# A decay table read backwards in place of its copy, other PSUM banks for the first two attention tiles, and a new order of loads and moves

## The chip, the cores and the metric

The kernel runs on one core of one Trainium2 chip. The metric is the device time of one execution in microseconds (us). The core has five instruction queues: PE (matmul), DVE (vector), ACT (scalar), POOL (GpSimd) and SP, which here issues every DMA. Each queue is worked off in order; an instruction waits for the data and the buffers that it needs.

## The reference

Three layers, one behind the other, in float32: an attention with decay, a layer with a gate, and a mixture of experts with soft routing.

```python
# attention: q, k, v are (2, 8, 768, 64), lam is (8,), worked off in blocks
for b in range(nb):
    intra = np.einsum('bhic,bhjc->bhij', qb, kb) * Dmask[None]   # lam ** (i - j) below the diagonal
    intra = np.einsum('bhij,bhjd->bhid', intra, vb)
    inter = np.einsum('bhid,bhde->bhie', qb * lam_pow[None], kv_state)
    out[:, :, sl] = intra + inter
    kv_state = lam_block[None, :, None, None] * kv_state + np.einsum('bhsd,bhse->bhde', kb * rev_pow[None], vb)
# gate: x (1536, 512), w_in (512, 2048), w_out (2048, 512)
h = x @ w_in
g = h * np.clip(h + 3.0, 0.0, 6.0) / 6.0
x = g @ w_out
# soft mixture: phi (512, 32), w1 (8, 512, 1024), w2 (8, 1024, 512); 4 slots an expert
logits = x @ phi
d = softmax of logits over the 1536 tokens;  slot_input = d.T @ x
slot_out[e] = np.maximum(slot_input[e] @ w1[e], 0.0) @ w2[e]
c = softmax of logits over the 32 slots;  out = c @ slot_out
```

## The kernel before

The 1536 tokens are twelve tiles t of 128 (six per batch); two neighbours make a pair tp. The 2048 columns of w_in are four parts n of 512.

*Attention* of a tile: pt are the transposed q and k, which ACT copies to tr; ps are the scores (two banks); DVE multiplies them with the decay table `dec` into pm; px is the output, from pm and v and, but for the first tile of a batch, from trd (q times powers of lam) and the state; pv is the state's increment, from v and from kd, k times the table's last column, which POOL makes. x is px in two parts for exact products.

*The decay table* holds, for each of 128 rows and 8 heads, 128 powers. DVE computes the powers (pw), copies them reversed into rp, SP stores rp to DRAM (pw_d) and reads it back with an offset of one element a row: dec_r (512 KB). ACT then copies dec_r, reversed, to dec.

*The gate*: w_in and w_out come as raw integer pairs (wraw, wo_raw). Two operations on ACT and two on DVE make floats of a block of 128 x 512 (tmp_i, tmp_o; "shift" is the last of them on DVE); for w_in ACT and POOL split them into whi and wlo. h of (t, n) is an h unit: two halves of six matmuls each, the first of which needs the first two k-blocks of part n. ACT and DVE make g of it. w_out times phi becomes w2s: transposes pwo, products w2p, for each n.

*The logits* of a pair and part n are lg, from w2s and from g with its tokens in the other layout. For pairs 0 to 4 the layout is changed by a move: DVE transposes blocks (gb), SP writes them to DRAM (gd, four transfers) and reads them back (gq). For pair 5 PE and ACT do it (pg, gt). All of them wait for every w2s. softmax (lr, dn, pd) collects the token sums as pairs come in; after the last pair psi gives the slots' input, and the experts run: p1 with w1, po with w2, whose weights (e, 64 transfers of 512 KB) SP loads into slots that come free.

*Memory*: 49 slots of 4 KB a partition in SBUF (the ring) hold nearly everything; the eight banks of PSUM are tagged h (2), s (2), x, g, l and d (one each). pt, ps and pv all take s; pwo and pg take g, lg takes l, w2p, pd and psi take d.

*The order* is fixed before the program is built. Every step is an `op` with an engine, a cost, its needs, a priority and the slots that it takes and frees; `Plan.run` goes through time with those costs and issues, on each engine, the ready step of the least priority (within `stick`, one that suits PE's mode). CFG holds the numbers that steer it: `order` (the sequence of h for pairs of tiles and parts n), `loads` (the first loads on SP, which follow each other strictly: q, k, v of a tile; t all three of them; W four blocks of w_in; o a block of w_out; P the store of the powers, D the table, p phi), `lead`, `wlead`, `wo`, `lg`, `sm` (what is added to a priority), `lres`, `pres`, `ares` (slots held back), `depth` (how many logits of earlier moves a block transposition lets stand open), and `eff` (the share of 360 GB/s at which a transfer is counted). The costs and waits in the plan set the order only; at run time an instruction waits for data and buffers.

Of the kernel before, what the change touches and what calls it, by code (L numbers as in the profile page):

```python
# [22 lines left out]
    bydma=(0, 1, 2, 3, 4),  # L23
    mv=-1034.0,
    mres=1,
    depth=6,
    warm=(1, 6, 5),
    order='00 01 10 11 02 03 12 13 20 22 21 23 30 31 32 33 40 41 42 51 43 50 52 53',
    stick=2.75,
    loads='q0 k0 P0 q1 D0 v0 k1 t2 p0 W0 v1 W1 v3 o8 q3 k3 W2 o9 t5 o10 o4 o6 o7 o5 k4 q4 v4 W3 o3 o0 o13 o1 o11 t6 t11 o12 o2 t9 t8 t7 o14 o15 t10',  # L30
    lead=5.5,
    wlead=-3.75,
    wo=7.0,
    lg=-9.5,
    sm=-9.25,
# [161 lines left out]
def attn_moe_softmoe_kernel(  # L197
# [23 lines left out]
    C = 128  # L221
# [23 lines left out]
    def rtile(shape, name, dt=F32):  # L245
        return ring.tile(shape, dt, tag=f"R{plan.slots['R'].pop(0)}", name=name)
# [147 lines left out]

    pw_done = op("DVE", 10, lambda: None, prio=-2000)

    def load_dec():
        T["dec_r"] = rtile([128, H, C], "dec_r")
        SP.dma_start(
            out=T["dec_r"],  # L400
            in_=bass.AP(pw_d.tensor, pw_d.offset, [[1, 128], [2 * C, H], [1, C]]),
        )

    rp_buf = Buf("R", 1, (1,))
    for item in CFG["loads"].split():
        i = int(item[1:])
        if item[0] in "qkv":
            load_qkv(item[0], i)
        elif item[0] == "t":
            for x in "qkv":  # L410
                load_qkv(x, i)
        elif item[0] == "w":
            load_w_in(i // 4, i % 4)
        elif item[0] == "W":
            for kt in range(KT):
                load_w_in(i, kt)
        elif item[0] == "p":
            ops["phi"] = load(load_phi, 65536, eff=0.4)
        elif item[0] == "P":
            ops["pw_d"] = load(store_pw, 8192, deps=[pw_done], rel=[rp_buf])  # L420
        elif item[0] == "D":
            ops["dec_r"] = load(
                load_dec, KB512, deps=[ops["pw_d"]], take=[ring_buf("dec_r")], eff=0.65
            )
        elif item[0] == "o":
            load_wo_raw(i)
        else:
            for kk in range(4 * i, 4 * i + 4):
                load_wo_raw(kk)

    def make_dec():
        T["dec"] = rtile([128, H, C], "dec")
        r = T.pop("dec_r")
        ACT.copy(
            T["dec"], bass.AP(r.tensor, r.offset + C - 1, [list(r.ap[0]), [C, H], [-1, C]])
        )

    def lamq_products():
        T["lamq_p"] = ptile("x", [128, NPAIR, C], "lamq_p")
# [6 lines left out]
    def make_lamq():  # L449
# [179 lines left out]
    def attention(t, prio):  # L632
# [214 lines left out]
    def logits(tp, n, prio):  # L847
# [61 lines left out]
        if tp in BY_DMA:  # L909
# [570 lines left out]
```

## Time and profile before

| | |
|---|---|
| runs | 321.19, 323.36 and 326.72 us, median 323.36 |
| the profiled execution | 323.14 us, span in the profile 321.0 us |
| busy in the span | PE 288.5 us, DVE 180.5, ACT 131.6, POOL 48.9 |
| moved by DMA | 93.30 MB |
| chain of waits, by engine | PE 57%, DMA 23%, DVE 9% |

The span is what the profile covers. A busy PE is one with a matmul in flight; since matmuls are pipelined, the share says where PE stood still and not how fast it was. The chain of waits is followed back from the last instruction, at each step to what released it.

### The profile page before, as it was taken

The page shows a single profiled execution, that of the slowest core. Times are in us where ns is not written, and L with a number is a line of the kernel's source. Part 1 is how long each engine was busy: PE and PEld are TensorE (multiplying, and loading weights), DVE is VectorE, ACT ScalarE, POOL GpSimd, SP SyncE. Part 2 cuts the span into 40 slices and gives each one's busy share as a digit, 9 for nine tenths or more (in the row PEclk, how much of TensorE's full clock was granted, in tenths as well). Part 3 has the DMA queues.
Part 4 walks back from the last instruction along what each step waited for, and adds up shares of the span by engine and source line. Part 5 has one row for each costly group of instructions (what it writes and reads, how often), then busy time and mean ns, then how long its engine had stood idle before and what let it go on. Part 6 is the DMA issues. An engine that isn't in the chain of part 4 may idle for free.

```text
span 321.0 us, 6470 instructions
## 1 busy us (share of the span) xinstructions
PE 288.5 (90%) x2532; PEld 211.7 (66%) x2532; DVE 180.5 (56%) x338; ACT 131.6 (41%) x239; POOL 48.9 (15%) x62
## 2 busy tenths in 40 slices
PE   4667969999999999998899699999999988899782
PEld 3456858888888788886556275776787556566341
DVE  5167899999662264774399636457432516530032
ACT  2258969799555345231223121234233331112032
POOL 5126751352511101200100010000000010000000
PEclk9997999999999999999999899999999999999978
DMA  4999999998859705398889999978989999999977
GB/s 92 234 354 361 327 305 313 387 293 236 221 144 246 205 0 127 77 271 284 273 266 311 302 351 378 372 245 255 317 248 415 418 420 418 418 414 414 383 270 259
DMA packets 76318, 93.30 MB, mean 291 GB/s; under 512 B 41976, under 2 KB 60416, under 8 KB 76288
## 3 DMA queue, kind: packets, MB, share of 16 engines
q1 hardware_dynamic: 76288, 92.89, 86.3%
q8 instruction: 20, 0.33, 0.4%
q14 instruction: 10, 0.08, 0.1%
HBM read 75.04 MB, written 17.83 MB: 289 GB/s over the span
## 4 chain that ended last, share of the span: by engine, by line
PE 57%; DMA 23%; DVE 9%; SPq 4%; issue 3%; ACT 2%; DVEq 0%
PE h L799 31%; DMA e<-in_moe_w_dram 9%; DMA gq<-gd 7%; DMA gd<-gb 5%; PE ps L677 4%; PE px L713 3%; SPq L883 3%; PE lg L903 3%; PE pwo L590 2%; PE px L708 2%; PE pt L646 2%; PE pd L999 2%; DVE gb L874 2%; DMA dec_r<-pw_d 2%; PE pg L856 1%
## 5 line engine op out<-in xcount | busy, mean ns | idle before, releaser
L799 PE MATMUL h<-whi,x 128*128 128x512 f32 x384 | 123.8, 404 | 1.8 <-DVE g L819 1.7
L799 PEld LDWEIGHTS h<-whi,x 128*128 128x128 f32 x384 | 68.4, 188 | 19.7 <-issue 3.6
L799 PE MATMUL h<-wlo,x 128*128 128x512 f32 x192 | 75.3, 392 | 0.0
L813 ACT ACTIVATE g<-h,half_b 128x512 f32<-128x512 f32 x48 | 33.0, 688 | 74.3 <-PE h L799 72.9
L819 DVE SCALAR_TENSOR_TENSOR g<-g,h 128x512 f32<-128x512 f32 x48 | 32.8, 684 | 48.7 <-ACT g L813 47.6
L799 PEld LDWEIGHTS h<-wlo,x 128*128 128x128 f32 x192 | 36.0, 188 | 8.1
L874 DVE STREAM_TRANSPOSE gb<-g 128x1024 f32<-128x1024 f32 x20 | 24.6, 1236 | 6.0 <-PE px L713 3.0
L529 POOL TENSOR_TENSOR wlo<-tmp_i,whi 128x512 fp32r<-128x512 f32 x16 | 21.6, 1360 | 27.4 <-ACT whi L526 27.3
L731 POOL TENSOR_TENSOR state<-state,lamq 64x256 f32<-64x256 f32 x16 | 10.2, 639 | 89.2 <-PE px L708 60.0
L685 DVE TENSOR_TENSOR pm<-ps,dec 128x512 f32<-128x512 f32 x24 | 15.7, 683 | 13.5 <-PE ps L677 7.8
L677 PE MATMUL ps<-tr 64*128 64x128 f32 x192 | 16.7, 323 | 3.9 <-ACT tr L657 3.9
L677 PEld LDWEIGHTS ps<-tr 64*128 64x128 f32 x192 | 14.1, 222 | 8.1 <-ACT tr L657 5.1
L657 ACT COPY tr<-pt 128x512 f32<-128x512 f32 x24 | 13.8, 593 | 13.3 <-PE pt L646 9.1
L502 DVE SCALAR_TENSOR_TENSOR tmp_i<-tmp_i 128x512 int32<-128x512 int32 x16 | 16.9, 1064 | 2.2 <-ACT tmp_i L488 2.1
L903 PE MATMUL lg<-gq,w2s 128*32 128x256 f32 x160 | 13.1, 401 | 4.9 <-DMA gq<-gd 4.8
L1333 PE MATMUL po<-e,ht 128*32 128x256 f32 x256 | 15.9, 397 | 1.3 <-DMA e<-in_moe_w_dram 1.3
L646 PE MATMUL pt<-ident,qk 128*128 128x128 f32 x96 | 15.6, 300 | 1.3 <-DVE pm L685 1.1
L713 PE MATMUL px<-pm,vd 128*64 128x128 f32 x192 | 14.6, 292 | 2.4 <-DVE pm L685 2.4
L666 POOL TENSOR_TENSOR vd<-qk,dec 128x512 f32<-128x512 f32 x10 | 11.8, 1182 | 25.1 <-DMA qk<-in_k_dram 17.5
L1299 PE MATMUL p<-e,sim 128*32 128x256 f32 x256 | 14.2, 380 | 1.3 <-DVE sim L1182 1.3
L646 PEld LDWEIGHTS pt<-ident,qk 128*128 128x128 f32 x96 | 11.9, 153 | 4.8 <-issue 2.1
L713 PEld LDWEIGHTS px<-pm,vd 128*64 128x64 f32 x192 | 11.2, 143 | 4.3 <-DVE pm L685 3.0
(107 smaller groups left out, 349.0 us busy)
## 6 DMA issues: line engine op xcount, KB each, us to landing
e<-in_moe_w_dram SPq DMA_DIRECT2D x64, 512.0 KB, 9.7
gd<-gb SPq DMA_DIRECT2D x80, 128.0 KB, 4.6
gq<-gd SPq DMA_DIRECT2D x20, 512.0 KB, 5.1
wraw<-in_moe_w_in_dram SPq DMA_DIRECT2D x16, 512.0 KB, 5.9
wo_raw<-in_moe_w_out_dram SPq DMA_DIRECT2D x16, 512.0 KB, 7.7
wo_d<-wo_f SPq DMA_DIRECT2D x32, 128.0 KB, 2.4
wo<-wo_d SPq DMA_DIRECT2D x8, 512.0 KB, 7.2
qk<-in_q_dram SPq DMA_DIRECT2D x12, 256.0 KB, 4.4
```

Source lines behind the costliest of these rows:

```text
L502: DVE.scalar_tensor_tensor(out=lw if dst is None else dst(), in0=hp, scalar=3, in1=lw, op0=ALU.logical_shift_left, op1=ALU.bitwise_or,)
L529: POOL.tensor_tensor(out=T["wlo", n, kt // 2][:, kt % 2], in0=T.pop(("tmp", key))[:, 1].bitcast(F32), in1=T["whi", n, kt // 2][:, kt % 2]. ...
L646: PE.transpose(p[:, a], x[:, i, 2 * a : 2 * a + 2].rearrange("p a d -> p (a d)"), ident,)
L677: PE.matmul(ps[g][:, p], lhsT=y[r, 1, p], rhs=y[r, 0, p], start=True, stop=True)
L685: DVE.tensor_tensor(out=T["pm", t].rearrange("p (a g) c -> p g a c", g=2)[:, g], in0=T["ps", t][g], in1=T["dec"].rearrange("p (a g) c -> p ...
L713: PE.matmul(px[64 * h2 : 64 * h2 + 64, p], lhsT=vd[:, 0, h], rhs=P[:, h], start=c == 0, stop=c == 0 or p == NPAIR - 1,)
L799: PE.matmul(ph, lhsT=xt[:, a, kt], rhs=T[w, n, part][:, kt % 2], start=i == 0, stop=i == 3 * KT - 1,)
L813: ACT.activation(T["g", tp, n][:, i], T["h", t, n], AF.Relu, bias=half_b, scale=1.0 / 6.0)
L819: DVE.scalar_tensor_tensor(out=to, in0=to, scalar=1.0, in1=T.pop(("h", t, n)), op0=ALU.min, op1=ALU.mult,)
L874: DVE.transpose(out=x.rearrange("p q c i t -> p i c q t"), in_=T["g", tp, n].rearrange("p i (c q t) -> p i c q t", c=4, q=4),)
L903: PE.matmul(T["l", tp][32 * c4 : 32 * c4 + 32], lhsT=w2s[:, n, c4], rhs=rhs, start=n == 0, stop=n == NF - 1,)
L1333: PE.matmul(T["po", hf][32 * qd : 32 * qd + 32], lhsT=T["ht", e // 4][:, e % 4, b8], rhs=T["e2", e, b8 // 2][:, b8 % 2, lo:hi] if e < WHOL ...
```

## The change

The table is read where it lands: dec_r becomes dec, and `T["dec"]` is an access pattern over it that runs backwards, so that DVE (pm) and POOL (kd) read it with a negative step; ACT's copy and its slot are gone. For tiles 0 and 1 (`early=2`) pt of q, pt of k and pv take the banks g, l and d in place of s. The moves' `eff` become 0.72 and 0.98, `depth` 3, and the numbers in CFG others, among them `order` (n = 3 of tiles 4 and 5 earlier) and `loads`.

```diff
@@ -23,24 +23,25 @@
     bydma=(0, 1, 2, 3, 4),
     mv=-1034.0,
     mres=1,
-    depth=6,
+    depth=3,
     warm=(1, 6, 5),
...
-    loads='q0 k0 P0 q1 D0 v0 k1 t2 p0 W0 v1 W1 v3 o8 q3 k3 W2 o9 t5 o10 o4 o6 o7 o5 k4 q4 v4 W3 o3 o0 o13 o1 o11 t6 t11 o12 o2 t9 t8 t7 o14 o15 t10',
...
+    loads='q0 k0 P0 k1 v0 q1 D0 p0 W0 v1 t2 W1 v3 o8 q3 k3 W2 o9 o10 W3 o4 o6 o7 o5 k4 t5 q4 v4 o3 o0 o13 o1 t6 o12 o2 o11 t9 t7 t8 o14 o15 t10 t11',
...
-    ahead=17,
+    ahead=0,
     whole=6,
     ares=0,
+    early=2,
 )
 
 
@@ -394,12 +395,13 @@
 
     pw_done = op("DVE", 10, lambda: None, prio=-2000)
 
+
     def load_dec():
-        T["dec_r"] = rtile([128, H, C], "dec_r")
+        r = rtile([128, H, C], "dec")
         SP.dma_start(
-            out=T["dec_r"],
-            in_=bass.AP(pw_d.tensor, pw_d.offset, [[1, 128], [2 * C, H], [1, C]]),
-        )
+            out=r, in_=bass.AP(pw_d.tensor, pw_d.offset, [[1, 128], [2 * C, H], [1, C]])
+        )
+        T["dec"] = bass.AP(r.tensor, r.offset + C - 1, [list(r.ap[0]), [C, H], [-1, C]])
 
     rp_buf = Buf("R", 1, (1,))
     for item in CFG["loads"].split():
@@ -419,8 +421,8 @@
         elif item[0] == "P":
             ops["pw_d"] = load(store_pw, 8192, deps=[pw_done], rel=[rp_buf])
         elif item[0] == "D":
-            ops["dec_r"] = load(
-                load_dec, KB512, deps=[ops["pw_d"]], take=[ring_buf("dec_r")], eff=0.65
+            ops["dec"] = load(
+                load_dec, KB512, deps=[ops["pw_d"]], take=[ring_buf("dec")], eff=0.5
             )
         elif item[0] == "o":
             load_wo_raw(i)
@@ -429,14 +431,6 @@
                 load_wo_raw(kk)
 
 
-
-
-    def make_dec():
-        T["dec"] = rtile([128, H, C], "dec")
-        r = T.pop("dec_r")
-        ACT.copy(
-            T["dec"], bass.AP(r.tensor, r.offset + C - 1, [list(r.ap[0]), [C, H], [-1, C]])
-        )
 
     def lamq_products():
         T["lamq_p"] = ptile("x", [128, NPAIR, C], "lamq_p")
@@ -456,11 +450,6 @@
         "DVE", 600, make_lamq, deps=[ops["lamq_p"]], prio=-9, rel=[b_x],
         take=[ring_buf("lamq")],
     )
-    ops["dec"] = op(
-        "ACT", 950, make_dec, deps=[ops["dec_r"]], prio=-10, rel=[bufs["dec_r"]],
-        take=[ring_buf("dec")],
-    )
-
 
 
 
@@ -635,12 +624,15 @@
         prev = ops.get(("state", t - 1)) if c > 0 else None
         old, new = states[c % 2], states[(c + 1) % 2]
         b_tr, b_trd, b_pm = Buf("R"), Buf("R"), Buf("R")
-        b_q, b_k, b_s, b_v, b_x = Buf("s"), Buf("s"), Buf("s", 2), Buf("s"), Buf("x")
+
+        q_tag, k_tag, v_tag = "gld" if t < CFG["early"] else "sss"
+        b_q, b_k, b_v = Buf(q_tag), Buf(k_tag), Buf(v_tag)
+        b_s, b_x = Buf("s", 2), Buf("x")
         b_qk, b_vd = bufs["qk", t], bufs["vd", t]
 
         def f_tr(i):
             def fn():
-                p = T["pt", t, i] = ptile("s", [128, NPAIR, C], f"pt{t}_{i}")
+                p = T["pt", t, i] = ptile((q_tag, k_tag)[i], [128, NPAIR, C], f"pt{t}_{i}")
                 x = T["qk", t]
                 for a in range(NPAIR):
                     PE.transpose(
@@ -692,7 +684,7 @@
 
         def f_pv():
             vd = T["vd", t]
-            pv = T["pv", t] = ptile("s", [128, NPAIR, D], f"pv{t}")
+            pv = T["pv", t] = ptile(v_tag, [128, NPAIR, D], f"pv{t}")
             for h in range(H):
                 p, h2 = divmod(h, 2)
                 PE.matmul(
@@ -915,8 +907,8 @@
                 take=[b_gb], reserve=move_reserve,
             )
             ops["gb"] = o
-            o = load(f_move_out, KB512, [o], rel=[b_gb], n=4, prio=CFG["mv"], eff=0.82)
-            o = load(f_move_in, KB512, [o], take=[b_last], prio=CFG["mv"], eff=1.08)
+            o = load(f_move_out, KB512, [o], rel=[b_gb], n=4, prio=CFG["mv"], eff=0.72)
+            o = load(f_move_in, KB512, [o], take=[b_last], prio=CFG["mv"], eff=0.98)
         else:
             b_last, o = b_gt, None
             for i in range(2):
```

What that does to the order, at the places of which the prediction speaks. The first is the start. In these rows pt1_0 is q of tile 1, the last number in a name is the build's own. On SP, before, from the store of the powers to the first block of w_in:

```order
L393 DMA pw_d_90<-rp_77 8x256
L351 DMA qk1_141<-in_q_dram 128x8x64
L399 DMA dec_r_155<-pw_d_90 128x8x128
L351 DMA vd0_159<-in_v_dram 128x8x64
L351 DMA qk1_141<-in_k_dram 128x8x64
L351 DMA qk2_173<-in_q_dram 128x8x64
L351 DMA qk2_173<-in_k_dram 128x8x64
L351 DMA vd2_176<-in_v_dram 128x8x64
L390 DMA phi_b_127<-in_moe2_phi_dram 128x4x32
L364 DMA wraw0_0_179<-in_moe_w_in_dram 128x1024
```

and now:

```order
L394 DMA pw_d_90<-rp_77 8x256
L352 DMA qk1_141<-in_k_dram 128x8x64
L352 DMA vd0_143<-in_v_dram 128x8x64
L352 DMA qk1_141<-in_q_dram 128x8x64
L401 DMA dec_158<-pw_d_90 128x8x128
L391 DMA phi_b_127<-in_moe2_phi_dram 128x4x32
L365 DMA wraw0_0_164<-in_moe_w_in_dram 128x1024
```

k of tile 1 and v of tile 0 stand ahead of the table, and tile 2 behind w_in. On PE, before, behind the scores of tile 0:

```order
L677 MATMUL ps0_1_164<-tr0_157 128x128
L713 MATMUL px0_203<-pm0_193,vd0_159 64x128 x8
L698 MATMUL pv0_216<-vd0_159 64x64 x8
L646 MATMUL pt1_0_230<-ident_91,qk1_141 128x128 x4
L646 MATMUL pt1_1_246<-ident_91,qk1_141 128x128 x4
L677 MATMUL ps1_0_261<-tr1_239 128x128
```

and now:

```order
L669 MATMUL ps0_1_167<-tr0_160 128x128
L638 MATMUL pt1_0_187<-ident_91,qk1_141 128x128 x4
L638 MATMUL pt1_1_194<-ident_91,qk1_141 128x128 x4
L690 MATMUL pv0_223<-vd0_143 64x64 x8
L705 MATMUL px0_238<-pm0_216,vd0_143 64x128 x8
L669 MATMUL ps1_0_254<-tr1_201 128x128
```

The transposes of tile 1 stand ahead of pv and px of tile 0. The second place is the first moves, right behind the last w2s. On DVE, before (gb0_1 is pair 0, n = 1):

```order
L874 STREAM_TRANSPOSE gb0_0_1469<-g0_0_505 128x2x4x4x32
L744 TENSOR_TENSOR state0_123<-state0_123,pv7_1444 64x4x64 x2
L874 STREAM_TRANSPOSE gb0_1_1485<-g0_1_586 128x2x4x4x32
L724 TENSOR_TENSOR x7_1487<-px7_1456,x7_1487 128x512
L874 STREAM_TRANSPOSE gb0_2_1508<-g0_2_846 128x2x4x4x32
L819 SCALAR_TENSOR_TENSOR g2_3_1506<-g2_3_1506,h4_3_1418 128x512
L874 STREAM_TRANSPOSE gb0_3_1522<-g0_3_1023 128x2x4x4x32
L874 STREAM_TRANSPOSE gb1_0_1532<-g1_0_557 128x2x4x4x32
```

and now:

```order
L866 STREAM_TRANSPOSE gb0_0_1434<-g0_0_445 128x2x4x4x32
L866 STREAM_TRANSPOSE gb0_1_1442<-g0_1_588 128x2x4x4x32
L866 STREAM_TRANSPOSE gb0_2_1457<-g0_2_790 128x2x4x4x32
L811 SCALAR_TENSOR_TENSOR g2_2_1390<-g2_2_1390,h5_2_1423 128x512
L811 SCALAR_TENSOR_TENSOR g2_1_1484<-g2_1_1484,h4_1_1449 128x512
L866 STREAM_TRANSPOSE gb0_3_1492<-g0_3_935 128x2x4x4x32
L736 TENSOR_TENSOR state0_123<-state0_123,pv7_1494 64x4x64 x2
L716 TENSOR_TENSOR x7_1503<-px7_1471,x7_1503 128x512
L811 SCALAR_TENSOR_TENSOR g2_1_1484<-g2_1_1484,h5_1_1507 128x512
L866 STREAM_TRANSPOSE gb1_0_1565<-g1_0_648 128x2x4x4x32
```

Three blocks follow each other; g, the state and x stand between the later ones. On SP, before, from the first move on:

```order
L883 DMA gd0_0_1474<-gb0_0_1469 32x4x256 x4
L351 DMA vd10_1491<-in_v_dram 128x8x64
L883 DMA gd0_1_1501<-gb0_1_1485 32x4x256 x4
L883 DMA gd0_2_1517<-gb0_2_1508 32x4x256 x4
L890 DMA gq0_0_1535<-gd0_0_1474 128x1024
L883 DMA gd0_3_1543<-gb0_3_1522 32x4x256 x4
L890 DMA gq0_1_1570<-gd0_1_1501 128x1024
L883 DMA gd1_0_1575<-gb1_0_1532 32x4x256 x4
L883 DMA gd1_1_1589<-gb1_1_1549 32x4x256 x4
L890 DMA gq0_2_1611<-gd0_2_1517 128x1024
L890 DMA gq0_3_1620<-gd0_3_1543 128x1024
```

and now:

```order
L875 DMA gd0_0_1444<-gb0_0_1434 32x4x256 x4
L875 DMA gd0_1_1465<-gb0_1_1442 32x4x256 x4
L875 DMA gd0_2_1486<-gb0_2_1457 32x4x256 x4
L882 DMA gq0_0_1505<-gd0_0_1444 128x1024
L875 DMA gd0_3_1516<-gb0_3_1492 32x4x256 x4
L882 DMA gq0_1_1530<-gd0_1_1465 128x1024
L882 DMA gq0_2_1532<-gd0_2_1486 128x1024
L882 DMA gq0_3_1563<-gd0_3_1516 128x1024
L875 DMA gd1_0_1574<-gb1_0_1565 32x4x256 x4
L875 DMA gd1_1_1604<-gb1_1_1588 32x4x256 x4
```

The reads of n = 1, 2 and 3 of pair 0 stand in a row, ahead of the blocks of pair 1.

## Rows read from the trace of the kernel before

**Rows 1.** The page's 40 slices of the span, busy tenths of PE and of DMA.
```profile
PE   4667969999999999998899699999999988899782
...
DMA  4999999998859705398889999978989999999977
```

**Rows 2.** Stretches of 10 us: length, busy us (instructions) of PE, PEld, DVE, ACT, POOL; PE clock, DMA, GB/s.
```profile
0.00:10.00 10.00, 4.70 (x22) 4.11 (x24) 4.39 (x13) 2.66 (x4) 4.49 (x19) 1.00 0.49 115
10.00:20.00 10.00, 6.92 (x58) 5.58 (x56) 3.51 (x6) 3.10 (x5) 3.19 (x4) 1.00 1.01 270
20.00:30.00 10.00, 6.44 (x58) 5.43 (x58) 7.16 (x12) 8.45 (x15) 4.84 (x5) 0.83 1.07 395
...
40.00:50.00 10.00, 7.25 (x45) 5.34 (x44) 9.91 (x16) 7.09 (x13) 4.90 (x5) 1.00 1.02 326
...
70.00:80.00 10.00, 10.00 (x79) 8.26 (x77) 9.83 (x18) 10.00 (x19) 1.99 (x3) 1.00 0.86 245
```

**Rows 3.** Waits of PE: for whom, us in total, times, longest.
```profile
PE lg L903 <- DMA gq<-gd: 4.8, 4, 2.8
...
PE h L799 <- DVE g L819: 1.7, 1, 1.7
```

**Rows 4.** Timeline of the start: start us, us, engine, line, operation, [idle before it, releaser].
```profile
4.51 1.15 DVE L278 COPY rp<-pw 8x128 f32<-8x128 f32 x1
4.59 1.00 POOL L310 MEMSET state<- 128x512 f32 x2
...
11.87 1.04 ACT L437 COPY dec<-dec_r 128x1024 f32<-128x1024 f32 x1 [2.68 <-DMA dec_r<-pw_d]
12.95 1.29 DVE L685 TENSOR_TENSOR pm<-ps,dec 128x512 f32<-128x512 f32 x2 [5.55 <-ACT dec L437]
...
15.11 1.99 SPq L364 DMA_DIRECT2D wraw<-in_moe_w_in_dram  x4
...
17.05 2.03 PE L646 MATMUL pt<-ident,qk 128*128 128x128 f32 x8
...
19.60 0.68 ACT L481 ACTIVATE tmp_i<-wraw 128x512 f32<-128x512 f32 x1
...
30.46 0.73 PE L799 MATMUL h<-whi,x 128*128 128x512 f32 x2
```

**Rows 5.** Groups of DVE on the page: line, operation, count | busy us, mean ns.
```profile
L685 DVE TENSOR_TENSOR pm<-ps,dec 128x512 f32<-128x512 f32 x24 | 15.7, 683 | 13.5 <-PE ps L677 7.8
...
L502 DVE SCALAR_TENSOR_TENSOR tmp_i<-tmp_i 128x512 int32<-128x512 int32 x16 | 16.9, 1064 | 2.2 <-ACT tmp_i L488 2.1
```

**Rows 6.** o14 and o15: issue and last shift (timeline), first pwo behind (chain).
```profile
104.55 2.75 SPq L378 DMA_DIRECT2D wo_raw<-in_moe_w_out_dram  x2
...
119.01 0.69 DVE L502 SCALAR_TENSOR_TENSOR wo_f<-tmp_o 128x512 int32<-128x512 int32 x1
...
121.65 0.44 PE pwo L590 x4
```

**Rows 7.** Two moves (timeline), and pieces of PE work (chain of waits).
```profile
131.62 1.20 DVE L874 STREAM_TRANSPOSE gb<-g 128x1024 f32<-128x1024 f32 x1
...
144.78 0.64 PE L903 MATMUL lg<-gq,w2s 128*32 128x256 f32 x8
...
166.69 1.24 DVE L874 STREAM_TRANSPOSE gb<-g 128x1024 f32<-128x1024 f32 x1
...
183.02 1.08 PE L903 MATMUL lg<-gq,w2s 128*32 128x256 f32 x8 [2.80 <-DMA gq<-gd]
...
251.50 1.39 PE h L799 x6
...
253.47 1.72 PE pd L999 x16
```

**Rows 8.** The expert stream: SP's issues (timeline), the last DMA piece of the chain.
```profile
240.15 19.20 SPq L1085 DMA_DIRECT2D e<-in_moe_w_dram  x17
...
295.24 8.65 DMA e<-in_moe_w_dram
```

More of the change, by code (lines that the diff above doesn't have):

```diff
@@ L25 @@
     mres=1,
-    depth=6,
+    depth=3,
     warm=(1, 6, 5),
-    order='00 01 10 11 02 03 12 13 20 22 21 23 30 31 32 33 40 41 42 51 43 50 52 53',
-    stick=2.75,
-    loads='q0 k0 P0 q1 D0 v0 k1 t2 p0 W0 v1 W1 v3 o8 q3 k3 W2 o9 t5 o10 o4 o6 o7 o5 k4 q4 v4 W3 o3 o0 o13 o1 o11 t6 t11 o12 o2 t9 t8 t7 o14 o15 t10',
[L31 to L35, printed above, removed]
+    order='00 01 10 11 02 03 23 12 13 20 22 21 30 31 32 33 40 41 42 51 43 50 52 53',
+    stick=1.75,
+    loads='q0 k0 P0 k1 v0 q1 D0 p0 W0 v1 t2 W1 v3 o8 q3 k3 W2 o9 o10 W3 o4 o6 o7 o5 k4 t5 q4 v4 o3 o0 o13 o1 t6 o12 o2 o11 t9 t7 t8 o14 o15 t10 t11',
+    lead=4.5,
+    wlead=-1.5,
+    wo=8.0,
+    lg=-9.0,
+    sm=-11.25,
     lres=4,
-    pres=4,
+    pres=3,
     sto=-1069.0,
```

## The prediction

> **What bounds the kernel now.** I read the strip of 40 slices first, then the table of 10 us stretches, PE's waits, and the timeline of the places where PE stands still. In the strip [rows 1] PE is at 9 from the seventh slice on with few dips, and the DMA engines are at 9 in the last quarter. So the run has three parts: a start in which PE waits, a long stretch in which it hardly does, and a tail paced by the expert weights. The stretches size the first part: PE is busy 4.70, 6.92 and 6.44 us of the first three times 10 us, so 11.94 us are idle, and 2.75 more from 40 to 50 [rows 2]. Behind that the named waits are small: 4.8 us for moved g tiles in front of logits, and 1.7 us for a bank of h that DVE had not emptied [rows 3]. From 240 us on SP issues the last 49 expert transfers without a pause (17 in the row shown, 24 and 8 behind them), and the DMA part of the chain of waits ends with one that lands at 303.9 [rows 8]. That stream starts behind the move of g of the fifth tile pair, so it moves with PE's progress up to there; its length is bytes over a rate that is flat already. I take it that what PE gains ahead of about 236 us comes off the end, one for one, and that nothing else does.
>
> The run profiled took 323.14 us, its span 321.0: 2.1 us lie around it. The median of the runs is 323.36, so I work on 323.1 without a correction. The runs shown spread over 5.5 us; some 2% (6.5 us) is what a measurement of this kernel can tell from no change.
>
> **The copy of the decay table.** It took ACT 1.04 us, and pm of tile 0 started as it ended, at 12.95 [rows 4]. Alone, its removal is worth up to 1.08 us there (11.87 to 12.95). But the order of the loads takes it back: k1 and v0 now stand ahead of the table on SP, two transfers of 256 KB. The stretch from 10 to 20 us moved 270 GB/s [rows 2], so 0.52 MB are 1.9 us more before it lands. Estimate: pm of tile 0 starts at 12.95 - 1.1 + 1.9, near 13.7. Nobody pays these 0.8 us in full: tile 1's transposes now run on PE in the meantime (below).
>
> What reading backwards costs on DVE no row of a like instruction shows. The nearest for the operation is pm itself, 683 ns for 512 columns [rows 5]; for the direction, on ACT, the copy of the table, 1024 columns in 1.04 us. The only backward read on DVE is the copy into rp: 128 columns in 1.15 us [rows 4], 9 ns a column, which would make 512 columns 4.6 us. POOL's memsets of state run beside it, and it ends at 5.66, just behind their end at 5.59, so I read it as a wait and take 0 for each of the 24 pm; the other end is +3.9 us each.
> The Trainium skill (SBUF — State Buffer, section Who interferes with whom) has a rule that fits: a DVE copy in a two-port mode and a GpSimd instruction hold the shared ports for a whole instruction, and the later one blocks; a DVE instruction with one SBUF input outside those modes does not contend. By that rule the long row is the wait, and pm, with ps in PSUM, stays at 0.68 us; by the bare row the sum would grow by tens of us. The row's end agrees; the page Vector Engine (DVE) Microarchitecture Reference, section 5.1, lists operands with a negative step as not measured.
>
> **The start: banks, and the order of the loads.** Today tile 1's transposes follow px and pv of tile 0, since pt, ps and pv share two banks of one kind. They start at 17.05, 4.1 us after pm could begin [rows 4]. With banks g, l and d they stand right behind ps of tile 0, in the hole while the decay table is waited for. Those banks belong to wo's transposes, the logits and w2p, which in PE's order come only after h units of tiles 0 to 3, so I cost that at nothing; were one still in use, PE would wait for one eviction.
>
> The larger part is W0. Its four transfers are issued from 15.11, and ACT starts on the first at 19.60; the first h starts at 30.46 [rows 4], behind POOL's second wlo. Now q2, k2 and v2 stand behind W0: 0.79 MB less ahead of it, at 270 GB/s 2.9 us. So ACT starts near 16.7. From there to the first h it is 10.9 us today, with pt, ps and px of tiles 1 and 2 between; the new order puts ps of tile 2 behind the first two halves of h, and ACT has tile 1's two copies behind it by then. Bounds for this stretch: the 10.9 as it is, or about 8 us, which is eleven ACT operations of some 0.7 us (0.68 the one shown). So the first h stands between 24.7 and 27.6, a gain of 2.9 to 5.8 us.
>
> Whether it stays is up to DVE, busy 9.9 and 9.8 of 10 us in stretches between 40 and 80 [rows 2]. What DVE can win is what it idles between 10 and 30 us, 6.49 + 2.84 = 9.3 us; with pm at 13.7 some 3 us of it pass before it can start, so 6.3 are the upper end. Its shifts take 1064 ns in the mean, where pm with as many columns takes 683 [rows 5]: a share of that is waiting, and it does not go away. I take 4.5 us for the whole start, nearest to the middle of 2.9 and 5.8, with the 1.7 us wait for h inside it. The lower end is 1.5: DVE holds what it has.
>
> **wo, W3 and the order of h.** Counted in h units (12 matmuls, 2.8 us), w2p of n = 3 now comes after 21 and not 22.5 of them, so the logits can start 4.2 us earlier in PE's work. By itself that gains nothing, since units only change places with logits. W3 is loaded ahead of six other loads, at no cost that I see. But o14 and o15 keep their place late on SP, behind the same stores and loads: issued at 104.55, the last converted at 119.70, with pwo of n = 3 at 121.65 [rows 6]. PE would now reach that pwo at 121.65 - 4.2 - 4.5 = 113.0. If the conversion moves with all that stands ahead of it, nothing is late; if it stays, PE waits 6.7 us. The loads ahead are fed by slots that earlier work frees, so I take 0.5.
>
> **The moves of g.** depth and the new rates act on the order alone; at run time only data and buffers are waited for. Blocks of n = 0, 1 and 2 of the first pair now follow each other on DVE and the reads of n = 1, 2 and 3 on SP, where blocks of the next pair stood between. Today the first move takes from 131.62 to 144.78, 13.2 us; a slow one takes from 166.69 to 183.02, 16.3 us, and PE waits 2.80 for it [rows 7]. In the new order the PE work between the logits of one pair and those of the same n of the next, added up from halves of h at 1.39, pd at 1.72 and shorter pieces [rows 7], is 12 us in two places (n = 0 of pairs 0 and 1, n = 3 of 1 and 2), 14 to 17 in six, 20 and more behind. At 13.2 a move plus some 1.5 until DVE comes to it, waits remain at the short gaps, 2 to 3 us each, less where the first has already spread them: some 4, against 4.8 now. I take a gain of 0.5; the bounds are +4.8 (all waits gone) and, at 16.3 + 2 a move in all eight gaps (14.5 in the mean, two rounds of 3.8 us), 7.6 - 4.8 = 2.8 us of loss. `ahead` does nothing, since the reserve that it switches on is of 0 slots.
>
> **Sum.** 323.1 - 4.5 + 0.5 - 0.5 = 318.6 us.
>
> **Rivals.**
> *DVE holds the start back.* For: it is all but full from 40 to 80 with the same work. Against: it idles 9.3 us before. The start gives 1.5 and the moves nothing, 321.6; slow moves on top would give 324.4.
> *The waits for moves go as well.* For: fewer blocks queue on SP ahead of a read. Against: two gaps of only 12 us. 323.1 - 4.5 - 4.8 = 313.8.
> *o15 comes late.* For: its place on SP is unchanged, and PE gets there 8.7 us earlier. Against: its slots come earlier too. At the full price, 323.1 - 4.5 - 0.5 + 6.7 = 324.8, slower than before; it decides from 5 us of wait at that pwo on.
> *Backward reads are slow on DVE.* About 12 of the 24 pm fall where DVE is the bound: 12 x 3.9 = 47 us, 365 and up. For: the row of rp. Against: the memsets beside it, and ACT's row.
>
> **Chances.** Forecast (315.5 to 321) 0.50, DVE holds 0.18, waits go as well 0.19, o15 late 0.10, slow reads 0.03. The range of 311.5 to 324.5 leaves out the slow rivals at their price and the far end of the good one. Faster by over 2% means under 316.9: the third case and a third of the forecast, 0.35; slower by over 2% the last case and what o15 and slow moves could make together, 0.06; the rest 0.59.
>
> **What would show it.** pm of tile 0 near 13.7 at 0.68 us; tile 1's transposes ahead of tile 0's px; ACT's first activation on wraw near 16.7 and the first h between 24.7 and 27.6; PE's idle time of the first 50 us down from 14.7 to about 10; waits for gq near 4 us; no wait at pwo; the pauseless expert stream some 4.5 us earlier at an equal rate. I am wrong if pm is longer, if PE has new waits between 50 and 130 us, or if the end does not follow PE.

## The result, and the profile after

The changed kernel takes 312.85 us in the median of 4 runs (311.09 to 314.37), the kernel before 324.24 beside it (321.19 to 326.72, 4 runs). The ratio is 0.9677 with a 95% interval of 0.9579 to 0.9775: faster, by 10.5 us. The ratio leaves out the run of 326.72 us, a slow one; the medians as they stand differ by 11.4. In a second set of runs (e12 below) the ratio was 0.9627 (0.9583 to 0.9671). The profiled execution took 311.09 us, with a span of 309.3 against 321.0.

The 40 slices of the changed kernel, PE and DMA, to be laid beside [rows 1]:

```profile
PE   4689899999999999998999999999999988899972
DMA  3999999999879761787899999948999999999987
```

From the third slice to the 38th PE is at 8 or 9, where the third and the sixth were at 6, and the dip to 6 at the 23rd slice of [rows 1] is gone. The stretches say the same in numbers (length, busy us of PE, PEld, DVE, ACT, POOL, PE clock, DMA, GB/s), beside [rows 2]; the last line spans the whole stage of the moves:

```profile
0.00:10.00 10.00, 4.70 (x22) 4.10 (x24) 4.39 (x13) 2.66 (x4) 4.48 (x19) 1.00 0.54 123
10.00:20.00 10.00, 8.23 (x71) 7.01 (x68) 4.93 (x9) 5.27 (x9) 2.37 (x3) 1.00 1.04 324
20.00:30.00 10.00, 8.95 (x78) 7.20 (x79) 9.93 (x15) 7.90 (x15) 8.31 (x7) 1.00 0.98 303
30.00:40.00 10.00, 9.12 (x85) 7.20 (x84) 9.57 (x16) 9.70 (x18) 7.79 (x8) 1.00 1.05 361
40.00:50.00 10.00, 9.63 (x68) 7.60 (x67) 8.60 (x17) 9.84 (x18) 3.61 (x5) 1.00 1.02 414
...
130.00:250.00 120.00, 118.73 (x860) 81.79 (x857) 69.11 (x136) 33.62 (x65) 3.71 (x6) 1.00 0.92 322
```

PE's idle time in the first 50 us fell from 14.7 to 9.4 us. From 130 to 250 us it idles 1.3 us and the granted clock is 1.00 throughout. The same stretch of the kernel before:

```profile
130.00:250.00 120.00, 115.09 (x848) 81.04 (x846) 69.55 (x128) 30.29 (x58) 4.77 (x7) 0.99 0.88 296
```

There it was 4.9 us idle, and one ten of these us ran at a mean clock of 0.83, a loss of 1.7 us more.

The start in the timeline of the changed kernel, beside [rows 4]:

```profile
4.51 1.15 DVE L279 COPY rp<-pw 8x128 f32<-8x128 f32 x1
...
11.99 1.94 PE L638 MATMUL pt<-ident,qk 128*128 128x128 f32 x8 [0.67 <-DMA qk<-in_q_dram]
...
14.34 1.28 DVE L677 TENSOR_TENSOR pm<-ps,dec 128x512 f32<-128x512 f32 x2
...
15.40 0.67 ACT L470 ACTIVATE tmp_i<-wraw 128x512 f32<-128x512 f32 x1 [0.84 <-DMA wraw<-in_moe_w_in_dram]
...
24.89 0.71 PE L791 MATMUL h<-whi,x 128*128 128x512 f32 x2
```

Tile 1's transposes stand at 11.99 in place of 17.05 and fill the wait for the table; the first h is 5.6 us earlier. The two groups of [rows 5], from the page of the changed kernel, now with the table read backwards:

```profile
L677 DVE TENSOR_TENSOR pm<-ps,dec 128x512 f32<-128x512 f32 x24 | 15.7, 682 | 6.3 <-PE ps L669 6.0
...
L491 DVE SCALAR_TENSOR_TENSOR tmp_i<-tmp_i 128x512 int32<-128x512 int32 x16 | 15.2, 955 | 0.1
```

PE's waits (for whom, us in total, times, longest), beside [rows 3]:

```profile
PE lg L895 <- DMA gq<-gd: 1.3, 1, 1.3
PE pt L1394 <- DVE r L1377: 1.1, 1, 1.1
PE pv L690 <- POOL vd L658: 1.1, 1, 1.1
```

The waits for moved g went from 4.8 to 1.3 us. No wait of PE for pwo of n = 3 is among them. The moves and what follows, in the timeline, beside [rows 7]:

```profile
121.51 1.08 PE L595 MATMUL w2p<-wo_t,phi_b 128*32 128x128 f32 x32
...
134.99 1.24 DVE L866 STREAM_TRANSPOSE gb<-g 128x1024 f32<-128x1024 f32 x1
...
136.27 0.64 PE L895 MATMUL lg<-gq,w2s 128*32 128x256 f32 x8
...
142.82 0.64 PE L895 MATMUL lg<-gq,w2s 128*32 128x256 f32 x8 [1.27 <-DMA gq<-gd]
...
149.52 0.64 PE L895 MATMUL lg<-gq,w2s 128*32 128x256 f32 x8
...
260.06 3.70 PE L1153 MATMUL psi<-wo,ant 128*32 128x128 f32 x128 [0.18 <-DVE ant L1131]
```

And the expert stream on SP, beside [rows 8]; it starts 9.8 us earlier:

```profile
230.39 19.29 SPq L1077 DMA_DIRECT2D e<-in_moe_w_dram  x17
```

To split the gain I use three landmarks of each timeline: the end of the last w2p (n = 3), where the moves begin; the start of psi, where all logits are done; the end of the span. Because the order sets how many h units stand ahead of that w2p (22.5 before, 21 now), its time is also given for 21 units, at 2.8 us a unit.

| kernel | first h | w2p ends | for 21 units | psi starts | w2p (21) to psi | psi to end |
|---|---|---|---|---|---|---|
| before | 30.46 | 131.31 | 127.1 | 269.73 | 142.6 | 51.3 |
| changed | 24.89 | 122.59 | 122.6 | 260.06 | 137.5 | 49.2 |

So the start gave 4.5 us and the stage of the moves 5.1. The last column differs by 2.0. In this one execution of the kernel before the granted clock was 0.57 in the mean from 305 to 309 us, which is 1.7 us lost; in the 11 runs below in which the column was read it is 49.2 to 50.7, in those with the old order of the moves too. I leave it out, and 9.6 us remain, near the 10.5 of the ratio.

### The profile page after: what moved, and what is told of

The parts are those of the page before. It is cut to its first block, busy times and chain, and to the rows that moved or that the text cites. A ratio compares the mean times of both kernels' runs of the same rounds, so it can differ in the third digit from the quotient of the medians.

```text
span 309.3 us, 6464 instructions
## 1 busy us (share of the span) xinstructions
PE 285.8 (92%) x2532; PEld 212.9 (69%) x2532; DVE 178.7 (58%) x338; ACT 130.9 (42%) x238; POOL 50.8 (16%) x62
## 4 chain that ended last, share of the span: by engine, by line
PE 62%; DMA 12%; SPq 8%; DVE 8%; ACT 4%; issue 3%; POOL 2%; DVEq 0%; ACTq 0%; POOLq 0%
PE h L791 32%; DMA e<-in_moe_w_dram 6%; PE lg L895 4%; PE pd L991 4%; PE ps L669 3%; SPq L352 3%; PE px L705 3%; PE pt L638 3%; DMA gd<-gb 2%; PE px L700 2%; PE pwo L579 2%; SPq L1101 2%; DMA wraw<-in_moe_w_in_dram 2%; PE p L1291 2%; DMA gq<-gd 2%
## 5 line engine op out<-in xcount | busy, mean ns | idle before, releaser
L791 PEld LDWEIGHTS h<-whi,x 128*128 128x128 f32 x384 | 68.4, 188 | 21.5 <-issue 4.0
L518 POOL TENSOR_TENSOR wlo<-tmp_i,whi 128x512 fp32r<-128x512 f32 x16 | 22.7, 1428 | 20.8 <-ACT whi L515 15.9
L649 ACT COPY tr<-pt 128x512 f32<-128x512 f32 x24 | 13.7, 592 | 16.5 <-PE pt L638 14.8
L658 POOL TENSOR_TENSOR vd<-qk,dec 128x512 f32<-128x512 f32 x10 | 12.6, 1259 | 39.0 <-DMA qk<-in_k_dram 12.9
L669 PEld LDWEIGHTS ps<-tr 64*128 64x128 f32 x192 | 13.7, 210 | 4.5 <-issue 2.9
L1325 PE MATMUL po<-e,ht 128*32 128x256 f32 x256 | 14.8, 381 | 0.6 <-DMA e<-in_moe_w_dram 0.6
L491 DVE SCALAR_TENSOR_TENSOR tmp_i<-tmp_i 128x512 int32<-128x512 int32 x16 | 15.2, 955 | 0.1
L638 PEld LDWEIGHTS pt<-ident,qk 128*128 128x128 f32 x96 | 12.1, 154 | 4.5 <-issue 2.5
L491 DVE SCALAR_TENSOR_TENSOR wo_f<-tmp_o 128x512 int32<-128x512 int32 x16 | 11.7, 742 | 4.2 <-ACT tmp_o L477 4.0
L1291 PEld LDWEIGHTS p<-e,sim 128*32 128x32 f32 x256 | 12.0, 110 | 3.1 <-DVE sim L1174 1.6
```

The lines of the kernel that those rows point to most:

```text
L491: DVE.scalar_tensor_tensor(out=lw if dst is None else dst(), in0=hp, scalar=3, in1=lw, op0=ALU.logical_shift_left, op1=ALU.bitwise_or,)
L518: POOL.tensor_tensor(out=T["wlo", n, kt // 2][:, kt % 2], in0=T.pop(("tmp", key))[:, 1].bitcast(F32), in1=T["whi", n, kt // 2][:, kt % 2]. ...
L638: PE.transpose(p[:, a], x[:, i, 2 * a : 2 * a + 2].rearrange("p a d -> p (a d)"), ident,)
L669: PE.matmul(ps[g][:, p], lhsT=y[r, 1, p], rhs=y[r, 0, p], start=True, stop=True)
L791: PE.matmul(ph, lhsT=xt[:, a, kt], rhs=T[w, n, part][:, kt % 2], start=i == 0, stop=i == 3 * KT - 1,)
L1291: PE.matmul(p1[32 * j : 32 * j + 32], lhsT=T["sim"][:, e, b4], rhs=T["e1", e, b4][:, 256 * j : 256 * j + 256], start=b4 == 0, stop=b4 == 3,)
```

## The experiments

The runs e1 to e4, e5 to e8 and e9 to e12 shared a chip each, with runs of the kernel before on it. The table gives medians, the ratio to the kernel before, and the landmarks of the profiled execution (21 h units stand ahead of the last w2p in all but e3 with 21.5, e5 with 20.5 and e9 with 20).

| run | us | ratio, 95% | first h | w2p ends, 21 units | psi | w2p to psi |
|---|---|---|---|---|---|---|
| e1 moves undone | 321.08 | 0.9891 (0.9809 to 0.9973) | 23.94 | 122.6 | 269.81 | 147.3 |
| e2 moves alone | 320.95 | 0.9865 (0.9768 to 0.9962) | | | | |
| e3 banks undone | 318.33 | 0.9807 (0.9727 to 0.9887) | 31.03 | 126.8 | 266.11 | 139.3 |
| e4 loads alone | 324.72 | 1.0007 (0.9969 to 1.0046) | 22.73 | 129.8 | 273.41 | 143.6 |
| e5 banks alone | 325.72 | 1.0061 (1.0025 to 1.0097) | 30.63 | 132.2 | 274.56 | 142.4 |
| e6 rates undone | 317.34 | 0.9777 (0.9704 to 0.9849) | 24.18 | 123.6 | 268.10 | 144.5 |
| e7 depth undone | 311.79 | 0.9625 (0.9568 to 0.9682) | 24.12 | 123.6 | 259.95 | 136.4 |
| e8 loads first | 311.22 | 0.9609 (0.9548 to 0.9670) | 23.01 | 122.7 | 258.95 | 136.3 |
| e9 banks and loads | 319.24 | 0.9835 (0.9782 to 0.9888) | 27.90 | 123.8 | 268.36 | 144.6 |
| e10 copy back | 315.50 | 0.9717 (0.9666 to 0.9768) | 27.96 | 125.2 | 262.36 | 137.2 |
| e11 e8 with depth 6 | 311.24 | 0.9582 (0.9539 to 0.9624) | 23.84 | 123.8 | 260.57 | 136.7 |
| e12 changed, again | 312.55 | 0.9627 (0.9583 to 0.9671) | 24.59 | 123.1 | 260.93 | 137.8 |

One number of the CFG changes the whole plan behind the place where it first matters, so each of these kernels is another order, not the same one with one step taken out; that holds for every difference below. The three sets ran on different chips, so small differences between them are read from the ratios.

My theory after the result was that the gain is two halves: the start, as forecast, and the order of the moves, which I had put at 0.5. The rival was that the waits of the moves went because everything ahead of them had become earlier.

### e1: depth and rates of the moves undone

```diff
-    depth=3,
+    depth=6,
-            o = load(f_move_out, KB512, [o], rel=[b_gb], n=4, prio=CFG["mv"], eff=0.72)
-            o = load(f_move_in, KB512, [o], take=[b_last], prio=CFG["mv"], eff=0.98)
+            o = load(f_move_out, KB512, [o], rel=[b_gb], n=4, prio=CFG["mv"], eff=0.82)
+            o = load(f_move_in, KB512, [o], take=[b_last], prio=CFG["mv"], eff=1.08)
```

> The changed kernel with the old depth and rates of the moves (depth 6, eff 0.82 and 1.08); everything up to the first moves is issued in the changed kernel's order, so the first logits should stand near 136 us as there. Theory (the rates and the depth, by the order of the moves that they give, bring some 5 us of the gain, the start the other 5): 317 to 319 us, with the waits of logits for gq back at 3 to 5 us and stretches of PE at the lower granted clock or idle behind 140 us. Rival (the waits for the moves went because everything ahead of the moves is earlier and stands otherwise, whatever the depth): 312 to 314 us, as the changed kernel.

321.08 us. The start is as in the changed kernel (w2p ends at 122.55), and psi is 9.7 us later. The rival falls: with all else early, the old numbers of the moves give 147.3 us from w2p to psi, more than the kernel before. Its stage of the moves, and two of its stretches:

```profile
130.00:250.00 120.00, 113.07 (x811) 77.91 (x806) 66.95 (x134) 30.20 (x60) 3.70 (x6) 0.99 0.90 314
...
222.00:223.00 1.00, 0.54 (x8) 0.16 (x8) 0.00 (x0) 0.00 (x0) 0.00 (x0) 1.00 0.97 368
...
224.00:226.00 2.00, 2.00 (x10) 1.51 (x8) 1.29 (x2) 0.00 (x0) 0.00 (x0) 0.50 0.67 188
```

PE is idle for 6.9 us. What a wait can do beside its own length is in the timeline of this kernel, at the longest wait for a gq:

```profile
222.46 0.64 PE L895 MATMUL lg<-gq,w2s 128*32 128x256 f32 x8 [2.35 <-DMA gq<-gd]
223.03 1.62 PE L669 MATMUL ps<-tr 64*128 64x128 f32 x16
224.58 1.22 PE L791 MATMUL h<-whi,x 128*128 128x512 f32 x2
...
231.12 0.73 PE L791 MATMUL h<-whi,x 128*128 128x512 f32 x2
```

Two matmuls of h take 1.22 us right behind it and 0.73 later: the granted clock is 0.50, which is 1.2 GHz, from 224 to 226, and the ten us from 220 stand at 0.83 in the mean, 1.7 us lost.

### e2: depth and rates alone

The reverse edit of e1 on the kernel before.

> The kernel before with the new depth and rates of the moves alone (depth 3, eff 0.72 and 0.98), start unchanged: first h near 30.5 us, first logits near 144.8. Theory (the moves' order brings some 5 us by itself): 318 to 320 us, waits for gq 1 to 2 us in all, expert stream issued some 4 to 5 us earlier than 240. Rival (it does nothing without the earlier start and the new order of h): 322 to 325 us, waits for gq near 5.

320.95 us, 0.9865: the numbers of the moves give 4.4 us by the ratio without anything else (1.2 to 7.5 by its interval), near the theory's 5. Of this kernel only the time is used, since its profiled execution, 324.42 us, is the longest of its four.

### e6 and e7: which of the two numbers

e6 is the changed kernel with eff 0.82 and 1.08, e7 with `depth=6`.

> The changed kernel with the old rates of the moves (eff 0.82 and 1.08) and depth 3 kept. If the rates make the order that loses no time to the moves: 318 to 321 us, psi 6 to 9 us behind the changed kernel's 260.1, as in e1. If the depth makes it: 312 to 314, psi near 260 to 261.

> The changed kernel with depth 6 again and the new rates kept. If the depth makes the order that loses no time to the moves: 318 to 321 us, psi 6 to 9 us behind 260.1. If the rates make it: 312 to 314. If each gives a part: both this and e6 between 314 and 318.

e6 takes 317.34 us, e7 311.79. With the new rates, depth is worth nothing. The rates are worth some 5 us (e6 against e12, whose intervals lie apart), and the column w2p to psi shows it in every execution that was read: 136.3 to 139.3 us in the seven with the new rates (changed, e3, e7, e8, e10, e11, e12), 142.4 to 147.3 in the six with the old ones (before, e1, e4, e5, e6, e9). PE's waits for gq part in the same way: 0 to 1.6 us in all with the new rates, 3.5 to 5.6 with the old. PE in the stage of the moves of e7 does not stop at all:

```profile
130.00:250.00 120.00, 120.00 (x875) 82.67 (x874) 69.56 (x138) 34.00 (x66) 3.71 (x6) 1.00 0.93 324
```

How the rates do it is argued and not shown. A move that is counted longer should have its logits put later in PE's row, with more h ahead of them. The order fits this in part: between the last w2p and the first logits of pair 2 the plan puts 16 halves of h in the kernel before, in e1, e4 and e6, 18 in e7 and 19 in the changed kernel. But e5 and e9, with the old rates, have 20 and 17 there, and PE waits 5.2 and 4.4 us for gq in them all the same. Counted over all twenty moves, from the start of a block to its logits, there are 7.0 to 7.4 halves in the mean with the new rates and 6.1 to 6.5 with the old, but 7.1 in the kernel before. So the count alone does not settle it. e1 against e6 (0.9891 against 0.9777, intervals that overlap) leaves open whether depth matters under the old rates.

### e3, e4, e5 and e9: what the start consists of

e3 is the changed kernel with `early=0` (tiles 0 and 1 back in the banks of s), e4 the kernel before with the new `loads`, e5 the kernel before with the new banks, e9 with both:

```diff
-        b_q, b_k, b_s, b_v, b_x = Buf("s"), Buf("s"), Buf("s", 2), Buf("s"), Buf("x")
+        q_tag, k_tag, v_tag = "gld" if t < CFG["early"] else "sss"
+        b_q, b_k, b_v = Buf(q_tag), Buf(k_tag), Buf(v_tag)
+        b_s, b_x = Buf("s", 2), Buf("x")
```

> The changed kernel with the first two tiles' pt and pv back in the banks of tag s (early=0). Theory (the load order carries most of the start, the banks 1 to 1.5 us): 313.5 to 315 us, first h 1 to 2 us behind the changed kernel's 24.9. Rival A (the banks hide the whole of the later table, so without them the 4 us hole at tile 1's transposes is back): 316 to 318. Rival B (the banks are worth nothing): 312 to 313.

> The kernel before with the new order of the first loads alone (k1 and v0 ahead of the table, tile 2 behind the first blocks of w_in); the copy on ACT and the banks of tag s stay. Theory (W0 ahead of tile 2 is the larger part of the start): first h between 25 and 28 us in place of 30.5, time 319 to 321. Rival (without the other banks and with the copy the later table eats what the earlier W0 gains): first h near 29 to 30, time 322 to 325.

> The kernel before with the other banks for pt and pv of the first two tiles, and nothing else (loads, copy, moves as before). After e3 and e4 the theory is that the banks carry the start: PE idles some 4 us less in the first 50 us, w2p of n = 3 ends some 4 us earlier than 131.3, time 319 to 321. Rival (the banks pay only together with the new order of the loads, since tile 1's k is loaded too late in the old one): w2p within 1.5 us of 131.3, time 323 to 325.

> The kernel before with the other banks and the new order of the first loads, both, and nothing else. Loads alone (e4) and banks alone (e5) gave nothing. Theory (they pay together: k1 is there in time and has a bank, so that tile 1's transposes fill the wait for the table, and W0 is there when they are done): w2p of n = 3 ends 4 us earlier than 131.3 at an equal count of h units, 319 to 321 us. Rival (the gain of the start needs the order that the whole set of numbers gives): 323 to 326 us, with PE at the lower granted clock somewhere between 10 and 60 us as in e4 and e5.

Each theory of one carrier fell. The banks undone cost 5.5 us against the changed kernel by medians, just above the range of rival A, whose hole the rows below show. Not all of that is the hole: PE's idle time of the first 50 us is 11.1 us against 9.4, and 2.6 us more are two waits for pwo near 75 us, which the changed kernel does not have. But alone the banks cost 0.6%, and the loads alone give nothing, although the first h of e4 starts at 22.73, 7.7 us earlier than before. Only both together gain, 5.7 us by medians (e9), with the copy still there, and w2p 3.3 us earlier. That is the theory's time, although the clock fell once as the rival had it (0.83 from 20 to 30 us). Without the banks, PE waits for pm, and tile 1's transposes come behind; the timeline of e3:

```profile
14.52 2.35 PE L705 MATMUL px<-pm,vd 128*64 128x128 f32 x15 [3.21 <-DVE pm L677]
...
17.87 1.11 PE L638 MATMUL pt<-ident,qk 128*128 128x128 f32 x4
...
31.03 0.71 PE L791 MATMUL h<-whi,x 128*128 128x512 f32 x2
```

and with banks and loads, e9:

```profile
11.58 1.94 PE L650 MATMUL pt<-ident,qk 128*128 128x128 f32 x8 [0.27 <-DMA qk<-in_q_dram]
...
27.90 0.72 PE L803 MATMUL h<-whi,x 128*128 128x512 f32 x2
```

In e4 the early h runs first and the attention behind it waits. One of these waits in its timeline:

```profile
45.62 0.69 PE L698 MATMUL pv<-vd 128*64 128x64 f32 x16 [2.05 <-ACT tr L657]
```

and the stretch around it, with 2.8 us idle and the lower clock for a part:

```profile
40.00:50.00 10.00, 7.24 (x68) 6.06 (x67) 9.89 (x18) 9.82 (x18) 5.04 (x5) 0.81 1.02 410
```

In e5 PE idles 16.6 us up to 130 us, 1.9 more than before (2.6 us are again waits for pwo), and the clock is the other loss, in this one execution; one stretch of it:

```profile
20.00:30.00 10.00, 8.28 (x58) 7.14 (x58) 8.02 (x12) 6.95 (x12) 4.39 (x3) 0.52 1.06 388
```

At 0.52 over 8.28 busy us, some 4 us of work at full clock are lost.

### e8 and e11: the loads still earlier, and the memset moved

```diff
-    loads='q0 k0 P0 k1 v0 q1 D0 p0 W0 ...
+    loads='q0 k0 k1 v0 q1 P0 D0 p0 W0 ...
-        POOL.memset(st, 0.0)
+        DVE.memset(st, 0.0)
```

> The changed kernel with k1, v0 and q1 issued ahead of the store of the powers, into time in which SP's queue stood waiting for rp, and with the memset of the state on DVE in place of POOL. Theory (the table lands 1 to 2 us earlier, and pm of tile 0 with it; rp took 1.15 us because of the memset beside it, so it falls to 0.2 to 0.4 us): rp 0.2 to 0.4 us, pm of tile 0 at 12.5 to 13.3 in place of 14.3, first h near 24, time 310.5 to 312. Rival A (POOL's memset had nothing to do with it, reading backwards is slow): rp stays near 1.1 us. Rival B (the first 25 us are paced by W0 and not by the table): time 312 to 314, as the changed kernel.

> e8 (k1, v0, q1 ahead of the store of the powers, memset of the state on DVE) with depth 6 as in e7. Both stood near 311.5. If their small gains add: 309.5 to 311 us, and faster than the changed kernel run beside it by 0.5% or more. If they were the spread of the runs: within 0.3% of the changed kernel.

The timeline of e8:

```profile
4.50 0.21 DVE L279 COPY rp<-pw 8x128 f32<-8x128 f32 x1
4.77 1.02 DVE L311 MEMSET state<- 128x512 f32 x2
...
23.01 0.71 PE L791 MATMUL h<-whi,x 128*128 128x512 f32 x2
...
36.53 0.63 PE L638 MATMUL pt<-ident,qk 128*128 128x128 f32 x4 [1.36 <-issue]
```

its stretch from 30 to 40 us:

```profile
30.00:40.00 10.00, 8.64 (x84) 7.12 (x83) 9.31 (x17) 9.69 (x18) 6.63 (x6) 1.00 1.06 391
```

and, in the timeline of the changed kernel, the same transposes:

```profile
36.76 0.63 PE L638 MATMUL pt<-ident,qk 128*128 128x128 f32 x4 [0.43 <-PE pt L638]
```

With no memset on POOL beside it the backward copy takes 0.21 us in place of 1.15: the long row was a wait. The first h is 1.9 us earlier, and at 36.5 both kernels are level again, in a stretch in which DVE is busy 9.31 and ACT 9.69 of 10 us; w2p ends at 122.69 against 122.59. That points to ACT and DVE, and not PE, as what paces the start from there on; it is argued and not shown. The table was there 1.9 us earlier (POOL reads it at 12.08, where it was 13.93), as the theory had it, but pm of tile 0 only 0.7 (at 13.62). e8 took 311.22 us. e11, with depth 6 added, took 311.24 beside the changed kernel's 312.55 (e12) on the same chip: 0.4% less, six runs from 310.35 to 311.88 against 311.66 to 313.89, with intervals of the ratios that overlap. It is the fastest of these kernels by its ratio, but a gain of 0.4%, between the two cases, is not established.

### e10 and e12: the copy put back, and the changed kernel again

```diff
-        T["dec"] = bass.AP(r.tensor, r.offset + C - 1, [list(r.ap[0]), [C, H], [-1, C]])
+    def make_dec():
+        T["dec"] = rtile([128, H, C], "dec")
+        r = T.pop("dec_r")
+        ACT.copy(
+            T["dec"], bass.AP(r.tensor, r.offset + C - 1, [list(r.ap[0]), [C, H], [-1, C]])
+        )
```

> The changed kernel with ACT's copy of the table put back. The copy takes 1.04 us of ACT behind the table's landing, so pm of tile 0 starts near 15.4 in place of 14.3. If DVE and ACT pace the stretch from 25 to 80 us whatever the first h does (as e8 suggests): 312 to 313.5 us, as the changed kernel. If the copy stands on the path: 313.5 to 315.

> The changed kernel itself, beside e10 and e11 on the same chip, so that differences under 1% can be read: 311 to 314.5 us, PE idle near 9 to 13 us in the first 50 us, no low granted clock ahead of 290 us.

e10 takes 315.50 us, 3.0 more than e12 beside it; the intervals of the two ratios just touch. Its timeline:

```profile
14.10 1.05 ACT L438 COPY dec<-dec_r 128x1024 f32<-128x1024 f32 x1
15.18 1.29 DVE L689 TENSOR_TENSOR pm<-ps,dec 128x512 f32<-128x512 f32 x2 [1.11 <-ACT dec L438]
16.35 1.12 PE L702 MATMUL pv<-vd 128*64 128x64 f32 x16 [2.76 <-POOL vd L670]
...
27.96 0.71 PE L803 MATMUL h<-whi,x 128*128 128x512 f32 x2
```

pm is later by the copy, about 1 us. PE waits 2.76 us for vd, which POOL makes from the table too, but that wait was 1.10 us in the first profile of the changed kernel and 2.34 in e12, so it does not explain the difference. The first h comes 3 us later, and w2p ends at 125.2, 2.0 us behind e12. So the copy stood on the path, with a time just above the second case's range. That it costs more than its own length is likely, and where the rest arises is not shown.

e12 had 11.2 us of idle time in the first 50 us, as expected, but the clock did fall ahead of 290 us: it was 0.83 in the mean from 10 to 20.

## Why the prediction came out as it did

The measured 312.85 us lies in the range of 311.5 to 324.5, but some 6 us below the forecast of 318.6 and outside the forecast's own case (315.5 to 321). What came is the rival *the waits for moves go as well*, to which I gave 0.19. So the range held because it took that rival in, and not because the sum was right.

**The copy and the backward reads.** The step held: pm takes 682 ns where it took 683, so reading backwards costs nothing. The reason given for the long row of rp, the memsets beside it, is shown by e8 (1.15 to 0.21 us). The Trainium skill (SBUF — State Buffer, section Who interferes with whom) has the rule of the shared ports by which a DVE copy in a two-port mode and a GpSimd instruction wait for each other; the trace agrees that one waits, with these two numbers. Which of the two came first, and so should go on, it does not settle: the copy starts at 4.51 and the memsets of state at 4.59, with another memset on POOL up to 4.53. The Trainium skill's page Vector Engine (DVE) Microarchitecture Reference, section 5.1, lists the negative step as not measured; here it is, for this one shape. pm of tile 0 was forecast near 13.7 and stood at 14.34. The copy itself was worth some 3 us by e10, where I allowed it 1.08; the intervals of e10 and e12 just touch.

**The start.** The total was right: 4.5 us forecast, 4.5 measured at the landmark (4.0 in e12); ACT began on W0 at 15.40 (forecast 16.7), the first h stood at 24.89 (24.7 to 27.6), the idle time of the first 50 us at 9.4 us (about 10; 11.2 in e12). Its division was not, so that it agrees to a tenth is luck. I called W0's earlier load the larger part and gave the banks no gain of their own. e4 has W0 at the same time (ACT begins on it at 15.08) and gains nothing. Banks and loads hold only together: a bank for tile 1, and its k and v in time. A term was left out, too: in the kernel before the clock stood at 0.83 from 20 to 30 us [rows 2], up to 1.7 us lost, and in the changed kernel it did not fall there. The landmark also leans on the 2.8 us a unit, since it counts 1.5 units more before. And the first h is not the landmark that pays: e4's is the earliest of all, and e8's lead of 1.9 us is gone at 36.5. In this the rival *DVE holds the start back* may have been right about what limits, ACT beside DVE, and was wrong about how much it leaves. Nor did the waiting of the shifts stay, as I had it: they take 955 ns in the mean, 1064 before.

**The moves.** This is the term that failed: "I take a gain of 0.5". The stage gave 5.1 us by the landmarks; from 130 to 250 us PE idles 3.6 us less, and 1.7 us less are lost to the clock. Two steps of the working were wrong. The first is the time that I gave a move: the PE work between the logits of a pair and the same n of the next, 12 us at the shortest, against 13.2 and 1.5. It supposes that a block waits for those logits. In the changed kernel the block of n = 0 of pair 1 starts at 134.99, 1.3 us ahead of the logits of pair 0 at 136.27; its own logits come at 149.52, 14.5 us later, without a wait. So the two short gaps, from which I forecast 2 to 3 us of wait each, had none; the one wait left, 1.27 us, is for n = 3 of pair 0. The second is that I weighed depth and rates together as a reshuffle of DVE and SP, worth next to nothing. The rates alone took some 3 us of waits for gq off PE (4.6 in e6, 1.3 in the changed kernel), and the lower clock behind such waits; that they do it by more halves of h ahead of the logits is argued (e6 and e7). The rival *the waits for moves go as well* gave 313.8 and is what happened. Its reason, fewer blocks queued on SP ahead of a read, is not needed: in e7 the writes of two blocks stand between the reads of pair 0 on SP (8 transfers from 135.00), and PE does not wait.

**What a wait costs.** I priced waits at their own length. In the kernel before the 2.80 us at 183.02 [rows 7] had the clock at 0.50 behind it:

```profile
183.00:186.00 3.00, 2.98 (x24) 1.98 (x24) 0.00 (x0) 0.00 (x0) 0.00 (x0) 0.50 0.96 309
```

3 us at 1.2 GHz, where full speed is 2.4: 1.5 us lost, half the wait once more. My upper bound of +4.8 for "all waits gone" left this out; with 1.3 us of waits still there, the stage gave 5.1.

**wo, o15 and the end.** o15 came in time: no wait at pwo. The 0.5 for it was not needed. That the end follows PE one for one held: from psi to the end it is 49.2 to 50.7 us in the changed kernel and the 11 runs read, whatever stood ahead (51.3 before), and the stream kept its rate (19.29 us for 17 issues, 19.20 before).

**Do the parts add?** By the ratios, banks and loads in the kernel before gave 5.4 us (e9), the moves alone 4.4 (e2), the copy 2.9 (e10 against e12), together 12.7, where the whole gave 10.5 and 12.1. But the moves undone from the changed kernel cost 7 to 8.6 us, well over what they gave alone, so the sum is no proof of independence. The part of the other numbers in CFG (`order`, `stick`, `lead`, `wlead`, `wo`, `lg`, `sm`, `pres`) and of the table's own `eff` (0.65 to 0.5) was not run by itself.

## What to carry to other kernels

Where an order is planned from costs, the rate assumed for a transfer can change the whole order behind it; lower rates for the moves were worth some 5 us here, with the same instructions, and PE waited less for what they moved. A wait on PE can cost more than its length, by a stretch at the lower clock behind it; whether there is one is read from the rows, since the length of the wait does not tell. An earlier load and a free bank were each worth nothing alone and 5.7 us together; judge them at a late landmark, with the count of work ahead of it, and not at the first instruction that moves.

## What was not expected of the hardware

PE's granted clock fell to 0.50 behind waits of 2.80 us (before), 2.35 (e1) and 1.69 (e6, 0.50 from 176 to 178 us), and not behind one of 1.27 (changed kernel). But the length does not decide it: there was no fall behind 2.12 us in the same e6 (the ten us from 138 stand at 1.00), nor behind 3.89 in e4 (up to 15.21; from 15 to 25 at 1.00). In the first 10 us PE idles 5.3 us in every one of these executions, and the ten us behind stand at 1.00 in all but e5 (0.80) and e12 (0.83). What decides it stays open.
